# Row tiles 2 and 3 normalised in 64-row halves, tiles 4 and 5 without quarter folding, W1's upper copy loaded once

## The chip, the cores and the metric

The kernel runs on one core of a Trainium2 chip. The time is the device time of one execution in microseconds (us); lower is better. The core has a matrix engine (PE, with its weight loader shown as PEld), a vector engine (DVE), a scalar engine (ACT), GpSimd (POOL) and SyncE (SP), which here only issues transfers. Each engine works through its own queue in order and waits on semaphores for the others. On-chip data lie in SBUF (128 partitions); matmul results land in PSUM, eight banks of 128 x 512 float32 values.

## The reference

The input x has 2048 rows of 448 bf16 values. Two kinds of layer alternate, twice each:

```python
def _A_ref(x, w_r, w_i):                      # spectral layer
    X = rfft2(x)                              # over 2048 rows and 448 columns
    return irfft2(X * (w_r + 1j * w_i))
def _B_ref(x, w1, b1, w2, b2):                # feed-forward layer, 448 -> 1792 -> 448
    h = x @ w1 + b1
    r = where(h > 0, h, 0)
    return (r * r) @ w2 + b2
x = x + _A_ref(_layernorm(x), A_w_r, A_w_i)
x = x + _B_ref(_layernorm(x), B_w1, B_b1, B_w2, B_b2)
x = x + _A_ref(_layernorm(x), A_w_r, A_w_i)
x = x + _B_ref(_layernorm(x), B_w1, B_b1, B_w2, B_b2)
```

The layer normalisation takes the mean and the variance of each row; it has no learned scale.

## The kernel before, in words

The 2048 rows form 16 row tiles of 128 rows (row 16p + t lies in partition p of tile t). Everything stays in SBUF from the first load to the last store. One pass consists of a spectral layer and a feed-forward layer, and the kernel makes two passes.

The spectral layer is a chain of small matmuls against constant matrices. `first_A` (or `second_A` in the second pass) does a part of the transform over rows, `stage_TD` the transform over the 448 columns (called d), `stage_B` the rest of the rows, `stage_W` multiplies by the spectral weights on DVE, and `stage_Bi` begins the inverse. The end of the inverse works tile by tile, two tiles at a time from tile 2 on: `stage_TI` (line 1087) is the inverse transform along d, whose result ACT or DVE copies from PSUM to `TIo`; `stage_AI` (line 1109) is the last step over rows, after which DVE adds the result to x (line 1146). For tiles with `t >= LATE[L]`, here 4, both steps use "quarter folding": `stage_TI` computes only 112 of 224 columns per matmul, four DVE operations of sums and differences (lines 1124 and 1127) make the rest, and `stage_AI` then streams 224 columns per matmul where it otherwise streams 448.

The feed-forward layer begins with `ln_B` (line 1164). It sums the squares of each row (line 1170) and takes a square root on ACT. Then there are two ways. Tiles 0 to 3 are left unnormalised: the standard deviation is written into two spare columns beside x, so that the matmul adds b1 times the deviation, and the layer's result is scaled afterwards with `r2`, the squared reciprocal. Tiles 0 and 1 are transposed on PE (`flip`), tiles 2 and 3 by a transposing transfer on SP's queue. Tiles 4 to 15 go through `ln_rows` (line 1211): reciprocal, one scaling per tile (on ACT or DVE), a copy of the last 64 columns, and the transposing transfer into `yT`. The array has 128 rows, and 448 columns of x make three blocks of 128 and one of 64.

The first matmul of the layer, called h, works on a chunk of four tiles and 14 blocks of W1's columns. For chunk 0 it is `h_part` (line 1266), on two tiles (256 columns) at a time, with four full-height matmuls per block, of which the fourth has data in half of its rows only. For the other chunks it is `h_pairs` (line 1226), on four tiles (512 columns), with seven matmuls of 64 rows per block; the matmuls of two blocks alternate between the lower and the upper half of the array. The upper half needs W1's last 64 rows a second time, in partitions 64 to 127: that copy is `W1u`, which before lies in the memory of `VT` (the inverse's work tensor) and is loaded by two transfers on SP's queue in each pass, after tile 6's transpose. ACT evicts each block with a ReLU (line 1277 or 1254, recorded as line 700), DVE squares it (recorded as line 735), and `o_tile` (line 1280) multiplies each tile by W2 in 14 matmuls and adds x on DVE (line 1292).

The order of each engine's instructions is written out in full. Work is cut into units, each engine's order is a list of unit numbers in `ORDER` (line 115), and `_Sched.schedule` (line 349) follows these lists; the costs and priorities in the code serve only where no list is given. Where its costs leave a long gap on PE, the planner also puts in dummy matmuls on `ones` (line 1415) to keep PE's activity up. Because the numbers are given in the order in which units are created, any change of the code renumbers all later units.

```python
# before, line 1369: chunk 0, two tiles at a time
for t0, t1 in ((0, 2), (2, 4)) if c == 0 else ():
    h_part(c, range(4 if t0 == 0 else 1), t0, t1)
    for fb in range(4 if t0 == 0 else 1, FB):
        h_part(c, (fb,), t0, t1)
```

## Time and profile before

| What | Value |
|---|---|
| time, median of 3 runs | 267.29 us (266.42 to 267.77) |
| the profiled execution's own time | 267.07 us |
| its span, first to last instruction | 265.1 us |
| PE busy | 257.7 us (97%) |
| DVE busy | 204.1 us (77%) |
| ACT busy | 172.8 us (65%) |
| share of PE in the chain that ended last | 80% |
| mean granted PE clock | 1.00 |

How to read the profile. The table of groups gives for each kind of instruction its engine, what it writes and reads, its shape, count, busy time, mean duration, and the idle time of the engine before it with what ended that. The chain that ended last is followed back from the last instruction: at each step to the instruction that released it. The timeline merges neighbouring instructions of one kind: start, time to the end of the last one, count. Nearly all matmuls are recorded under line 681, nearly all DVE operations on two tensors under 735, plain copies by ACT under 706 and by DVE under 707, so groups are told apart by their tensors: `ps<-yT,W_sb` is h, `ps<-yT,VT` is h with W1's upper copy, `ps<-W_sb,arena` is the second matmul, `ps<-TI_sb,VT` is `stage_TI` and `ps<-tmp,FI_sb` is `stage_AI`. In this kernel `arena` holds the squared h, the spectral work tensors and the normalised rows in turn.

### The profile page before, as it was taken

What the parts mean: (1) busy time and instruction counts of PE and PEld (TensorE: products, weight loads), DVE (VectorE), ACT (ScalarE), POOL (GpSimd) and SP (SyncE); (2) the same over time, 40 slices, a digit from 0 to 9 for tenths busy, and PEclk for the clock granted to TensorE, in tenths of its full rate; (3) what the DMA queues carried; (4) which work ended last, traced back from release to release, by engine and by line L of the source; (5) the groups of instructions that cost most, each with busy time, mean ns of one, the idle gap of its engine ahead of it and who ended that gap; (6) DMA issues with size and microseconds to landing.
All of it is one profiled execution on the core that took longest, in us unless ns stands there. A gap on an engine that the chain in (4) does not pass through costs nothing.

```text
span 265.1 us, 5674 instructions
## 1 busy us (share of the span) xinstructions
PE 257.7 (97%) x2127; PEld 163.0 (61%) x2127; DVE 204.1 (77%) x658; ACT 172.8 (65%) x375; POOL 14.3 (5%) x32
## 2 busy tenths in 40 slices
PE   8999989999999999999999999999999999999996
PEld 2686768797544555665558756789654465554454
DVE  3878998999969983489998899899964069921662
ACT  5887897999449447893216889999634886121820
POOL 8840000000000000000000000000000000000000
PEclk9999999999999999999999999999999999999999
DMA  7999700032300224000000000022232000220053
GB/s 226 383 262 350 262 3 2 0 72 41 74 2 1 42 39 80 2 0 2 0 1 2 2 0 2 0 45 41 42 69 45 2 0 2 40 41 2 0 176 104
DMA packets 25531, 16.33 MB, mean 62 GB/s; under 512 B 18174, under 2 KB 24542, under 8 KB 25504
## 3 DMA queue, kind: packets, MB, share of 16 engines
q1 hardware_dynamic: 24768, 14.25, 20.5%
q10 hardware_dynamic: 576, 0.92, 1.0%
q0 software_dynamic: 160, 0.81, 0.8%
q8 instruction: 17, 0.28, 0.5%
q14 instruction: 10, 0.08, 0.1%
HBM read 10.46 MB, written 1.84 MB: 46 GB/s over the span
## 4 chain that ended last, share of the span: by engine, by line
PE 80%; DVE 9%; ACT 6%; DMA 3%; issue 1%; SPq 1%; DVEq 0%
PE ps L681 80%; DVE tmp L735 6%; DMA xin<-in_A_x_dram 3%; DVE arena L735 2%; ACT VT L706 2%; ACT tmp L706 2%; ACT arena L706 2%; SPq L673 1%; DVE st L825 0%; ACT yT L706 0%; ACT mv L700 0%; PE ps L1415 0%; ACT Fs L717 0%; DVE VT L707 0%; DVE x_sb L1292 0%
## 5 line engine op out<-in xcount | busy, mean ns | idle before, releaser
L681 PE MATMUL ps<-yT,W_sb 64*128 64x512 bf16 (+1 forms) x770 | 90.3, 346 | 0.1
L681 PE MATMUL ps<-W_sb,arena 128*128 128x448 bf16 (+3 forms) x476 | 87.0, 342 | 0.0
L681 PEld LDWEIGHTS ps<-yT,W_sb 64*128 64x128 bf16 (+1 forms) x770 | 54.5, 95 | 31.9 <-ACT arena L700 1.3
L700 ACT ACTIVATE arena<-ps,b1col 128x512 bf16<-128x512 f32 x84 | 51.9, 689 | 28.7 <-PE ps L681 28.6
L681 PEld LDWEIGHTS ps<-W_sb,arena 128*128 128x128 bf16 x476 | 45.4, 98 | 38.5 <-DVE arena L735 1.5
L735 DVE TENSOR_TENSOR arena<-arena 128x512 bf16<-128x512 bf16 (+1 forms) x140 | 45.5, 362 | 24.7 <-ACT arena L700 24.5
L706 ACT ACTIVATE arena<-ps 128x448 bf16<-128x448 f32 (+1 forms) x41 | 26.0, 705 | 4.8 <-PE ps L681 4.7
L1170 ACT ACTIVATE VT<-x_sb 128x448 bf16<-128x448 bf16 x28 | 16.1, 579 | 16.6 <-DVE x_sb L1146 16.6
L700 ACT ACTIVATE mv<-mv,epst 128x1 f32<-128x1 f32 (+1 forms) x45 | 12.5, 296 | 17.0 <-DVE mv L826 14.0
L700 ACT ACTIVATE arena<-ps 128x256 bf16<-128x256 f32 x56 | 18.0, 386 | 0.6 <-PE ps L681 0.5
L681 PE MATMUL ps<-arena,G_sb 128*128 128x448 bf16 (+1 forms) x84 | 16.9, 335 | 0.9 <-ACT arena L706 0.9
L1292 DVE SCALAR_TENSOR_TENSOR x_sb<-ps,mv,arena 128x448 bf16<-128x448 f32 (+2 forms) x13 | 8.3, 643 | 12.0 <-PE ps L681 11.9
L706 ACT ACTIVATE XA<-ps 128x512 bf16<-128x512 f32 x26 | 14.2, 591 | 4.7 <-PE ps L681 4.7
L681 PE MATMUL ps<-H_sb,arena 128*128 128x256 bf16 x128 | 15.8, 273 | 1.2 <-DVE arena L735 0.6
L706 ACT ACTIVATE VT<-ps 128x1024 bf16<-128x1024 f32 (+2 forms) x20 | 14.0, 772 | 3.0 <-PE ps L681 3.0
L681 PE MATMUL ps<-yT,VT 64*128 64x512 bf16 x42 | 15.8, 376 | 0.0
L735 DVE TENSOR_TENSOR tmp<-arena,Wt 128x896 bf16<-128x896 bf16 x26 | 15.3, 620 | 0.6 <-ACT arena L706 0.4
L681 PEld LDWEIGHTS ps<-H_sb,arena 128*128 128x128 bf16 x128 | 11.7, 98 | 5.0 <-DVE arena L735 3.4
L681 PE MATMUL ps<-TD_sb,XA 112*128 112x112 bf16 (+3 forms) x232 | 14.4, 230 | 0.3 <-ACT arena L706 0.2
L681 PEld LDWEIGHTS ps<-TD_sb,XA 112*128 112x128 bf16 (+3 forms) x232 | 12.3, 103 | 3.1 <-ACT arena L706 0.8
L706 ACT ACTIVATE tmp<-ps 128x896 bf16<-128x896 f32 (+1 forms) x16 | 12.7, 853 | 1.1 <-PE ps L681 1.0
L681 PEld LDWEIGHTS ps<-arena,G_sb 128*128 128x128 bf16 x84 | 7.7, 98 | 6.5 <-ACT arena L706 1.5
(84 smaller groups left out, 299.0 us busy)
## 6 DMA issues: line engine op xcount, KB each, us to landing
out_dram<-x_sb SPq DMA_DIRECT2D x15, 112.0 KB, 1.8
W_sb<-in_B_w_dram SPq DMA_DIRECT2D x1, 1568.0 KB, 12.9
W_sb<-in_B_w_dram SPq DMA_DIRECT2D x1, 1344.0 KB
xin<-in_A_x_dram ACTq DMA_DIRECT2D x4, 224.0 KB, 5.2
xin<-in_A_x_dram SPq DMA_DIRECT2D x4, 224.0 KB, 7.2
H_sb<-c_H SPq DMA_DIRECT2D x1, 896.0 KB, 8.2
G_sb<-c_G SPq DMA_DIRECT2D x1, 672.0 KB, 9.5
Wt<-in_A_w_i_dram SPq DMA_DIRECT2D x1, 393.8 KB, 5.5
```

What stands on the lines that cost most here:

```text
L673: return e.dma_start(o, i)
L681: return sch.add("pe", lambda e: e.matmul(_res(o), lhsT, rhs, start=start, stop=stop, skip_group_check=skip), [lhsT, rhs], [o], cost=cost, ...
L700: sch.add("act", lambda e: e.activation(o, _res(i), func, **kw), rd, [o], cost=c)
L706: op = sch.add(engs[0], lambda e: e.activation(o, _res(i), ACT.Copy) if h[0].eng == "act" else e.tensor_copy(o, _res(i)), [i], [o], cost=c ...
L735: sch.add(eng, lambda e: e.tensor_tensor(o, _res(a), b, op), [a, b], [o], cost=_free(o) / rate + 69.0)
L1170: op = sch.add("act", lambda e, i=i, o=o, x=x, h=h: e.activation(o, x, ACT.Square, accum_out=sd[:, i, 1:2]) if h[0].eng == "act" else e.sc ...
L1292: small(lambda e: e.scalar_tensor_tensor(out=o, in0=_res(i), scalar=rs[0] if rs else 1.0, in1=xi, op0=ALU.add if t >= 4 and last else ALU. ...
```

## The change

Three things change, and all the order lists with them.

1. A constant `RAW = 2` takes the place of the 4 up to which tiles stay unnormalised. Tiles 2 and 3 now go through `ln_rows`, and their part of h goes through `h_pairs`, which gets the tile range as parameters: 64-row matmuls of 256 columns, evicted with b1 as a bias.
2. `LATE` goes from (4, 4) to (6, 6): tiles 4 and 5 take the way without quarter folding.
3. `W1u` becomes a tensor of its own, holds only the seven blocks that are read (every second one), and is loaded once at the start. The two transfers in each pass go away.

In the new lists the order differs in many places. In the first pass PE now does output tiles 0 and 1 before h of tiles 2 and 3, and h of tiles 4 to 7 directly after that, ahead of output tiles 2 and 3; tile 6's `stage_AI` comes before the first h. In the second pass h of tiles 2 and 3 follows h of tiles 0 and 1, then output tiles 3, 2, 0, 1, then h of tiles 4 to 11. Output tile 11 is the first pass's last, where before it was the second half of tile 15. In SP's list W1's two large parts and `W1u` come before the last part of `H_sb`, then W2, then `TI_sb`.

```diff
+RAW = 2
 ORDER = {
     "pe": """
...
-LATE = (4, 4)
+LATE = (6, 6)
...
-        W1u = VT[:].rearrange("p a b t c j -> p (a b) (t c j)")
+        W1u = sb("W1u", [P, FB // 2, P])
...
-        memset(x_sb[:, 0:4, D:4 * P].bitcast(FP32), 0.0, eng="pool")
+        memset(x_sb[:, 0:RAW, D:4 * P].bitcast(FP32), 0.0, eng="pool")
...
+        dma("sp", W1u[64:128], B_w1[384:448, :].rearrange("r (i k c) -> r i k c", k=2, c=P)[:, :, 1, :])
...
-            if t >= 4:
+            if t >= RAW:
                 ln_rows(t, n, last)
                 return
...
-            if t < 4 and last:
+            if t < RAW and last:
...
-        def h_pairs(c):
+        def h_pairs(c, t0, t1):
-            tk = slice(4 * c, 4 * c + 4)
+            tk, w = slice(4 * c + t0, 4 * c + t1), (t1 - t0) * P
...
-                w = W1u[h, fb // 4, fb % 4 * P:(fb % 4 + 1) * P] if up and j == 3 else W1_sb[h, j, f]
-                op = mm(q[fb][lambda b: ps[:, b, :]], w, yT[h, tk, j, :], start, stop, unit=u)
+                k = W1u[h, fb // 2, :] if up and j == 3 else W1_sb[h, j, f]
+                op = mm(q[fb][lambda b: ps[:, b, 0:w]], k, yT[h, tk, j, :], start, stop, unit=u)
...
-                    hb = hbuf[c % 2][:, fb, :]
-                    act(hb, q[fb][lambda b: ps[:, b, :]], ACT.Relu, bias=b1col[:, fb:fb + 1])
+                    hb = hbuf[c % 2][:, fb, t0 * P:t1 * P]
+                    act(hb, q[fb][lambda b: ps[:, b, 0:w]], ACT.Relu, bias=b1col[:, fb:fb + 1])
...
-            rs = [r2[:, t, 0:1]] if t < 4 else [mv2[:, t, 3:4]] if last else []
+            rs = [r2[:, t, 0:1]] if t < RAW else [mv2[:, t, 3:4]] if last else []
...
-                if t == 6:
-                    for k, w in ((0, 3), (3, 1)):
-                        dma("sp", W1u[64:128, k:k + w, 0:min(4 * P, FF - 4 * P * k)],
-                            B_w1[384:448, 4 * P * k:min(FF, 4 * P * (k + w))].rearrange("r (k c) -> r k c", k=w),
-                            after=[yT[:, 6, 0, :]])
...
-                    h_pairs(c)
-                for t0, t1 in ((0, 2), (2, 4)) if c == 0 else ():
+                    h_pairs(c, 0, 4)
+                for t0, t1 in ((0, RAW), (RAW, 4)) if c == 0 else ():
...
+                    if t0 > 0:
+                        h_pairs(c, t0, t1)
+                        continue
+                    h_part(c, range(4), t0, t1)
+                    for fb in range(4, FB):
```

More of the change, by code (lines that the diff above doesn't have):

```diff
@@ L1290, in o_tile @@
             i = q[lambda b: r(ps[:, b, 0:n])]
-            rs = [r2[:, t, 0:1]] if t < 4 else [mv2[:, t, 3:4]] if last else []
+            rs = [r2[:, t, 0:1]] if t < RAW else [mv2[:, t, 3:4]] if last else []
             small(lambda e: e.scalar_tensor_tensor(out=o, in0=_res(i), scalar=rs[0] if rs else 1.0, in1=xi,
-                                                   op0=ALU.add if t >= 4 and last else ALU.mult, op1=ALU.add),
+                                                   op0=ALU.add if t >= RAW and last else ALU.mult, op1=ALU.add),
                   [i, xi] + rs, [o], n / 0.96 + 128.0)
```

15 lines of the change are left out of this document (6 added, 9 removed), and 89 rows, old and new, of the table ORDER.

## The prediction

> **What bounds the kernel now.** I read the page's engine totals first, then the chain that ended last, then the engines' busy time stage by stage, and the timeline only where a stage showed idle time.
>
> ```profile
> span 265.1 us, 5674 instructions
> PE 257.7 (97%) x2127; PEld 163.0 (61%) x2127; DVE 204.1 (77%) x658; ACT 172.8 (65%) x375; POOL 14.3 (5%) x32
> ...
> 50.26 94.14 PE ps L681 x765
> ...
> 172.48 90.27 PE ps L681 x685
> ```
>
> The matrix engine PE is busy for 97% of the span, and two pieces of the chain, 94.14 and 90.27 us, are unbroken matmul work: there only a change in the number or rate of matmuls moves the end. What is left lies between those pieces. The stage table (columns: stretch and its length, then busy time of PE, weight loader, DVE, ACT, POOL, then clock and DMA) shows it:
>
> ```profile
> 30.00:42.00 12.00, 10.99 (x89) 8.04 (x88) 11.77 (x23) 10.16 (x14) 0.00 (x0) 1.00 0.14 52
> 42.00:50.30 8.30, 7.82 (x94) 6.23 (x93) 7.70 (x25) 7.46 (x15) 0.00 (x0) 1.00 0.01 2
> 50.30:65.00 14.70, 14.70 (x132) 12.61 (x133) 14.21 (x48) 14.11 (x47) 0.00 (x0) 1.00 0.25 51
> ...
> 150.00:162.00 12.00, 11.22 (x114) 7.81 (x112) 12.00 (x25) 10.38 (x15) 0.00 (x0) 1.00 0.00 0
> 162.00:173.00 11.00, 10.32 (x113) 8.07 (x111) 9.96 (x28) 10.01 (x17) 0.00 (x0) 1.00 0.01 1
> ```
>
> From 30 to 42 us and from 150 to 162 us DVE is full (11.77 of 12.00, 12.00 of 12.00): that is the multiplication by the spectral weights, which the diff leaves alone but for order. From 42 to 50.3 and 162 to 173 us (the ramps: inverse transform and normalisation of the first tiles until the feed-forward part starts) PE idles 0.48 and 0.68 us by the table, and waits somewhat longer than that, as its busy time counts the tails of matmuls. From 50.3 to 65 us PE is full, and DVE (14.21 of 14.70) and ACT (14.11) nearly are. So the change can act in three ways: by PE work, by the length of the two ramps, and by what falls late in the stretch after the first ramp. The granted clock is 1.00 in every row.
>
> **The change part by part.** The sum is made against the profiled execution, 267.07 us: span 265.1 and 1.97 around it. It lies 0.22 below the median of the three runs (267.29).
>
> First, the matmuls of tiles 2 and 3 in the first layer of the feed-forward part (14 blocks).
>
> ```profile
> 57.09 6.71 PE L681 MATMUL ps<-yT,W_sb 128*128 128x256 bf16 x60
> ...
> 76.66 1.67 PE L681 MATMUL ps<-yT,W_sb 64*128 64x512 bf16 x13
> 77.96 0.38 PE L681 MATMUL ps<-yT,VT 64*128 64x512 bf16 x1
> 78.17 1.67 PE L681 MATMUL ps<-yT,W_sb 64*128 64x512 bf16 x13
> ...
> 76.45 1.39 PEld L681 LDWEIGHTS ps<-yT,W_sb 64*128 64x128 bf16 x13
> ...
> 46.75 0.49 PEld L681 LDWEIGHTS ps<-TI_sb,VT 112*128 112x128 bf16 x8
> 46.85 0.56 PE L681 MATMUL ps<-TI_sb,VT 112*128 112x112 bf16 x8
> L681 PE MATMUL ps<-yT,W_sb 128*128 128x256 bf16 x224 | 25.9, 273 | 0.1
> ```
>
> Sixty 256-column matmuls take 6.71 us; without the last one's 0.273 that is 109.1 ns each. Today tiles 2 and 3 need 14 x 4 = 56 of them: 6.11 us. After, they need 14 x 7 = 98 matmuls of 64 rows, two at a time. At 512 columns such a pair takes (78.17 - 76.66) / 7 = 216 ns, the time of 512 columns streamed once, so the halves do run side by side. If they do at 256 columns too, 49 pairs at 109.1 ns take 5.35 us: 0.76 us less in each of the two passes. The doubt is the weight loads, two to a pair in half the time. Loads of 128 columns follow each other here every (0.49 - 0.098) / 7 = 56 ns, so even one after the other two take 112 ns: 5.49 us, a gain of 0.62. If pairs didn't overlap at all at this width, 98 x 109.1 = 10.69, a loss of 4.58. I take -0.76, because the rows of pairs are the nearest. The accumulation of a bank changes halves after four pairs of other work (0.44 us at this width); a matmul's 0.273 fits in that.
>
> By the Trainium skill, "TensorE: Matmul & The Clock Gate", section "LDWEIGHTS (loading the stationary operand)", a load takes its columns divided by 1.2 in ns whatever the rows, 107 ns for 128 columns; if the two loads of a pair went in sequence at that price, the pair would take 213 ns and the stage 49 x 213 = 10.5 us, 4.3 us more per pass (an estimate from that page). The trace disagrees on the rate: 56 ns between loads.
>
> Second, tiles 4 and 5 without quarter folding. The first step's eight matmuls get 224 columns in place of 112, the second step's four get 448 in place of 224.
>
> ```profile
> 46.46 0.55 PE L681 MATMUL ps<-tmp,FI_sb 128*128 128x224 bf16 x4
> ...
> 47.95 0.93 PE L681 MATMUL ps<-tmp,FI_sb 128*128 128x448 bf16 x4
> ...
> L681 PE MATMUL ps<-tmp,FI_sb 128*128 128x224 bf16 x64 | 8.6, 260 | 0.0
> L735 DVE TENSOR_TENSOR VT<-tmp 128x448 bf16<-128x448 bf16 x24 | 8.9, 382 | 0.1
> L735 DVE TENSOR_TENSOR tmp<-VT 128x448 bf16<-128x448 bf16 x24 | 8.6, 383 | 0.1
> L718 DVE TENSOR_SCALAR arena<-x_sb,rstd 128x448 bf16<-128x448 bf16 x15 | 4.7, 328 | 2.7 <-DMA yT<-arena 2.7
> L739 DVE COPY arena<-arena 128x128 bf16<-128x128 bf16 x12 | 2.3, 191 | 1.0 <-ACT arena L717 0.7
> ```
>
> The second step costs 0.93 - 0.55 = +0.38 us. A 224-column matmul takes (0.55 - 0.260) / 3 = 97 ns, a 112-column one (0.56 - 0.213) / 7 = 50 ns, so the first step costs 8 x 47 = +0.38. Together +0.76 per pass: what the halves give on PE, this takes back, and PE's own work stays as it is to within 0.1 us. On DVE four operations of 0.382 go, -1.53 us per pass; normalising tiles 2 and 3 adds two scalings (0.328), a copy (0.191) and a reciprocal (about 0.16) and drops four operations of about that length (two for the bias rows, two for the scale of the output), so DVE has about 1.2 us less per pass, in the stretch where it is nearly full.
>
> Third, W1's upper copy. It moves from two transfers in each pass to one transfer at the start (64 rows of 7 x 128 columns, 112 KB), queued on SP ahead of the last spectral constants.
>
> ```profile
> 70.10 1.31 SPq L673 DMA_DIRECT2D VT<-in_B_w_dram  x2
> ...
> VT<-in_B_w_dram SPq DMA_DIRECT2D x2, 192.0 KB, 3.3
> 42.74 1.75 PE L681 MATMUL ps<-TI_sb,VT 112*128 112x224 bf16 x22 [0.20 <-DVE VT L707]
> ```
>
> The 192 KB transfer landed in 3.3 us; I charge the new one at most that, in a start whose transfers are idle in the 30 to 42 us row but for a share of 0.14. The constant put last in SP's queue is the inverse matrix, first used at 42.74. Cost 0. The removed transfers held SP for 1.31 us in a pass, ahead of transposes for tiles that PE needs much later, so 0 there too; if the cover at the start went, it would cost up to 3.3.
>
> Fourth, ACT. The half-height path adds b1 as a bias on the eviction.
>
> ```profile
> L700 ACT ACTIVATE arena<-ps,b1col 128x512 bf16<-128x512 f32 x84 | 51.9, 689 | 28.7 <-PE ps L681 28.6
> L700 ACT ACTIVATE arena<-ps 128x256 bf16<-128x256 f32 x56 | 18.0, 386 | 0.6 <-PE ps L681 0.5
> L706 ACT ACTIVATE XA<-ps 128x512 bf16<-128x512 f32 x26 | 14.2, 591 | 4.7 <-PE ps L681 4.7
> ```
>
> With a bias 689 ns, without one 591 at the same size: 98 ns more, 14 times, 1.4 us of ACT per pass (0 at the lower end). Evictions overlap: 18.0 / 56 = 321 ns each, so about 419 with bias, against 5.35 / 14 = 382 that PE needs per block. ACT falls behind by 14 x 37 ns = 0.5 us, which the eight PSUM banks hold. Cost 0, up to 0.7 per pass if no bank is free.
>
> Fifth, the new order, which is where an unshown cost can be. In the first ramp the order puts tile 6's second step (0.38) and the longer tiles 4 and 5 (0.76) ahead of the first h matmul, and on ACT one more 896-wide eviction between the square roots and the transposed tiles' evictions.
>
> ```profile
> 43.74 4.96 ACT L706 ACTIVATE tmp<-ps 128x896 bf16<-128x896 f32 x6 [0.51 <-PE ps L681]
> 48.55 0.52 ACT L700 ACTIVATE mv<-mv,epst 128x1 f32<-128x1 f32 x2
> 48.92 1.58 ACT L706 ACTIVATE yT<-ps 128x384 bf16<-128x384 f32 x4
> ```
>
> Six such evictions take 4.96 us, 0.83 each. ACT would then reach the transposed tiles at about 48.55 + 0.52 + 0.83 = 49.9 and finish their two large pieces (0.45 each) at 50.8: h starts near 50.9 instead of 50.26, 0.64 later with 1.14 us more of PE work behind it. Gain 0.5; I take -0.4, as the small pieces come after a square on ACT. Bounds: -1.0 (all waiting in the ramp gone), +1.0 (nothing absorbed). In the second ramp by the same steps PE has 1.5 us more work ahead of h (0.76, and 0.76 of tiles 4, 14 pulled forward) and h starts about 1.65 later: +0.15, between -0.7 and +1.0. The stage with 64-row matmuls is entered once more in the second pass; around such a switch the loader idled 0.37 us, 0.19 of it under the last matmul:
>
> ```profile
> 74.92 0.54 PEld L681 LDWEIGHTS ps<-yT,W_sb 64*128 64x128 bf16 x7 [0.37 <-issue]
> 144.34 0.61 PE L1415 MATMUL ps<-ones 128*128 128x512 bf16 x2
> ```
>
> So about 0.1 a switch, +0.2 for two (0 to 0.4). The Trainium skill, "TensorEngine Tiling (Array Packing)", section "Key Properties", says that changing the tiling mode drains the engine; by that the switch has a price too, and the row agrees. Tiles 2 and 3 reach their transpose later, behind a reciprocal, two scalings and a copy:
>
> ```profile
> 53.44 1.34 SPq L668 DMA_TRANSPOSE yT<-x_sb  x1
> ...
> 176.03 1.23 SPq L668 DMA_TRANSPOSE yT<-x_sb  x1
> ...
> 172.95 0.27 PE L681 MATMUL ps<-yT,W_sb 128*128 128x256 bf16 x1
> ```
>
> In the first pass two output tiles (14 matmuls each) now stand between the h blocks of tiles 0, 1 and 2, 3, which leaves over 4 us. In the second nothing does: with the ramp's 1.65 and about 0.7 for the added steps the issue moves from 176.03 to about 178.4, the landing (3 us) to 181.4, and PE, which starts h at 172.95 + 1.65 = 174.6, gets there at 174.6 + 6.11 + 0.76 = 181.5. So it just fits: 0, up to +1.0.
>
> Between the passes the order ends the first on a whole tile (11) rather than on half of tile 15; PE fills there with dummy matmuls already (144.34), so the longer last chain shows: +0.1, between 0 and 0.6. The spectral stages keep their DVE work: 0, within 0.3.
>
> Sum: -1.52 + 1.52 - 0.4 + 0.15 + 0.2 + 0.1 = +0.05, so 267.1 us. Its own range is 265.8 to 268.4, this kernel's 0.5% (1.34 us), which is also about what a measurement can tell from no change.
>
> **The rivals.** Faster, because DVE binds the ramps. For it: DVE is at 7.70 of 8.30 and 9.96 of 11.00 there and loses 1.2 us in each pass. Against it: what it loses stood mostly after the critical squares, and ACT is just as full. If both ramps lost their waits, -1.0 and -0.7 in place of -0.4 and +0.15, and the 42 to 65 us stretch gave a further half us through earlier tiles, the time would be 265.1 to 265.6; I write 265.3.
>
> Slower, because tiles 4 to 7 come late. The order starts their h block straight after tiles 2 and 3, ahead of output tiles 2 and 3, and so about 6 us earlier than today (74.92), near 68.4. Their transposes are issued today at 60.64 and about 67:
>
> ```profile
> 60.64 7.64 SPq L668 DMA_TRANSPOSE yT<-arena  x2
> yT<-arena SPq DMA_TRANSPOSE x12, 3.0
> ```
>
> They land 3.0 us after issue. The second must be issued by 65.4; a count of DVE's operations ahead of it gives about 65.2. From there each us of DVE delay is one of PE: +1.5 us for a transpose issued at 67 as today gives 268.7. For it: DVE and ACT at 96% there. Against it: DVE's 1.2 us less.
>
> Slower, because ACT's bias paces the block in both passes: 2 x 0.7, 268.5. Slower by far, because pairs do not overlap at this width: 2 x (4.58 + 0.76) = +10.7, 277.8; the 512-column rows speak against it. The page's load rule would do the same at 2 x (4.3 + 0.76), 277.
>
> **How the numbers follow.** The forecast 0.47, DVE-bound ramps 0.28, late tiles 0.16, ACT's bias 0.06, no overlap 0.03. So faster by over 0.5% 0.28, within 0.5% 0.47, slower 0.25. The range 265.0 to 269.0 takes in the first two rivals' bounds and leaves out no overlap and the far ends.
>
> **What would show it.** Right: the 64-row matmuls of 256 columns at some 110 ns a pair; PE's busy time within 1 us of 257.7; h starting near 50.9 and 1.65 us later in the second pass. Wrong: PE waiting on a transpose or on ACT's evictions near 64 to 70 us; pairs over 115 ns; ramps shorter than today; or PE gaps before 42 us from late constants.

## The result and the profile after

Medians of twenty runs each on the same chips: 267.56 us after (267.29 to 268.60), 266.44 us before (266.20 to 267.77). The ratio is 1.0031, with a 95% interval from 1.0021 to 1.0041: the change costs 0.8 us by that ratio, 1.1 us between the two medians. The forecast was a difference of +0.05 us, and the interval leaves that out. That the absolute number, 267.1, came nearer than the difference is luck: its base lay high, as the profiled execution of before, 267.07 us, is 0.6 us above what that kernel takes in the median of twenty.

The page of the changed kernel, totals:

```profile
span 265.6 us, 5871 instructions
...
PE 256.6 (97%) x2212; PEld 160.0 (60%) x2212; DVE 202.1 (76%) x649; ACT 174.3 (66%) x375; POOL 14.1 (5%) x32
```

PE is busy 1.1 us less than before, DVE 2.0 us less, and the kernel is longer all the same. The chain that ended last (start, length, what) says where to look:

```profile
50.38 19.72 PE ps L680 x197
70.10 1.26 ACT arena L699 x2
71.41 69.91 PE ps L680 x525
141.34 1.57 ACT XA L705 x3
...
143.09 0.77 ACT XA L705 x2
143.91 0.90 PE ps L680 x20
...
167.12 95.89 PE ps L680 x794
```

Before, one piece of 94.14 us of matmuls reached from the first h to the end of the first pass. Now it is broken twice: at 70.10 by two of ACT's evictions, and at 141.34 by the chain at the end of the pass. The second pass is one piece of 95.89 us, longer than the 90.27 of before, as it now begins already in the ramp. The stage table (stretch, length, busy time of PE, weight loader, DVE, ACT, POOL, clock, DMA):

```profile
42.00:50.30 8.30, 7.94 (x92) 6.56 (x92) 7.88 (x24) 7.38 (x16) 0.00 (x0) 1.00 0.01 2
50.30:65.00 14.70, 14.63 (x130) 10.84 (x131) 14.24 (x51) 10.14 (x34) 0.00 (x0) 1.00 0.20 39
150.00:162.00 12.00, 11.78 (x124) 8.68 (x122) 12.00 (x25) 10.97 (x16) 0.00 (x0) 1.00 0.00 1
162.00:173.00 11.00, 10.16 (x104) 7.86 (x103) 10.51 (x27) 8.79 (x14) 0.00 (x0) 1.00 0.01 1
```

In the first of these stretches PE is busier than before (7.94 of 8.30, it was 7.82); ACT is relieved from 50 to 65 us (10.14, it was 14.11); the spectral stage is full on DVE as it was.

The two profiled executions can't be laid side by side by their clocks, because PE's first matmuls of the transform along d start at different times. The rows of that start and of the last matmuls, before:

```profile
17.52 1.76 PE L681 MATMUL ps<-TD_sb,XA 128*64 128x224 bf16 x32
...
257.81 4.93 PE L681 MATMUL ps<-W_sb,arena 128*128 128x448 bf16 x39
```

and after:

```profile
16.89 1.76 PE L680 MATMUL ps<-TD_sb,XA 128*64 128x224 bf16 x32
...
257.69 5.31 PE L680 MATMUL ps<-W_sb,arena 128*128 128x448 bf16 x41
```

From the start of the transform to the last matmul's end it is 257.81 + 4.93 - 17.52 = 245.22 us before and 257.69 + 5.31 - 16.89 = 246.11 after: +0.89. The start itself lies between 16.7 and 17.6 us in the kernels below, without any order among them, while three kernels whose PE work is the same (after, and the second and third experiment, e2_nobias and e4_squares) agree to 0.03 us in this length. So it is used from here on as the length of PE's work, cut into six stages by the start times of the matmuls named here (in us): transform up to the first matmul of `stage_TI`; first ramp up to the first h; h 1 up to the last first-step matmul of the next pass's spectral layer; spectral stage of the second pass; second ramp; second h to the end.

| Kernel | transform | ramp 1 | h 1 | spectral 2 | ramp 2 | h 2 | sum |
|---|---|---|---|---|---|---|---|
| before | 25.22 | 7.53 | 93.95 | 22.65 | 6.08 | 89.78 | 245.21 |
| after | 25.11 | 8.38 | 93.70 | 23.05 | 7.43 | 88.43 | 246.10 |
| e13_no_mix_only | 25.11 | 8.38 | 93.31 | 23.05 | 7.43 | 88.43 | 245.71 |
| e7_no_mix | 25.10 | 8.37 | 93.24 | 23.03 | 7.43 | 88.44 | 245.61 |
| e6_halves_last | 25.10 | 8.37 | 93.97 | 22.81 | 7.43 | 88.44 | 246.12 |
| e9_offload | 25.09 | 8.37 | 93.33 | 22.86 | 7.43 | 88.44 | 245.52 |
| e11_evac | 25.10 | 8.37 | 93.33 | 22.73 | 7.43 | 88.43 | 245.39 |
| p2_unfolded | 25.22 | 7.92 | 93.95 | 22.66 | 6.46 | 90.18 | 246.39 |
| p1_w1u_once | 25.22 | 7.52 | 93.95 | 22.66 | 6.08 | 90.48 | 245.91 |
| e12_folded | 25.10 | 8.13 | 95.47 | 22.72 | 7.33 | 89.88 | 248.63 |
| e3_order | 25.22 | 7.92 | 95.84 | 22.65 | 6.46 | 91.03 | 249.12 |

From the second ramp on the change gains nothing and loses nothing (ramp 2 and h 2 together 95.86 in both). The loss is made before: ramp 1 and h 1 together are 102.08 us after and 101.48 before, and spectral 2, which begins with what the end of the pass has left over, is 0.40 longer.

### The profile page after: what moved, and what is told of

The parts are those of the page before. It is cut to its first block, busy times and chain, and to the rows that moved or that the text cites. A ratio compares the mean times of both kernels' runs of the same rounds, so it can differ in the third digit from the quotient of the medians.

```text
span 265.6 us, 5871 instructions
## 1 busy us (share of the span) xinstructions
PE 256.6 (97%) x2212; PEld 160.0 (60%) x2212; DVE 202.1 (76%) x649; ACT 174.3 (66%) x375; POOL 14.1 (5%) x32
## 4 chain that ended last, share of the span: by engine, by line
PE 78%; DVE 15%; ACT 2%; issue 2%; DMA 1%; DVEq 0%
PE ps L680 77%; DVE tmp L734 9%; DVE arena L734 3%; DMA xin<-in_A_x_dram 1%; ACT arena L705 1%; ACT XA L705 1%; PE ps L1413 1%; DVE st L825 1%; DVE x_sb L1146 1%; DVE VT L706 1%; ACT arena L699 0%; DVE VT L1171 0%; DVE tmp L706 0%; DVE VT L734 0%; DVE arena L706 0%
## 5 line engine op out<-in xcount | busy, mean ns | idle before, releaser
L699 ACT ACTIVATE arena<-ps,b1col 128x512 bf16<-128x512 f32 (+1 forms) x112 | 63.7, 634 | 39.0 <-PE ps L680 38.8
L680 PE MATMUL ps<-yT,W_sb 64*128 64x512 bf16 (+2 forms) x840 | 88.7, 339 | 0.1
L680 PEld LDWEIGHTS ps<-yT,W_sb 64*128 64x128 bf16 (+1 forms) x840 | 51.2, 94 | 34.5 <-issue 1.9
L1292 DVE SCALAR_TENSOR_TENSOR x_sb<-ps,mv,arena 128x448 bf16<-128x448 f32 (+2 forms) x15 | 9.5, 649 | 14.0 <-PE ps L680 13.8
L705 ACT ACTIVATE XA<-ps 128x512 bf16<-128x512 f32 (+1 forms) x27 | 14.6, 585 | 7.7 <-PE ps L680 7.5
L680 PE MATMUL ps<-yT,W1u 64*128 64x512 bf16 (+1 forms) x56 | 19.6, 349 | 0.0
L699 ACT ACTIVATE mv<-mv,epst 128x1 f32<-128x1 f32 (+1 forms) x45 | 12.7, 299 | 9.6 <-DVE mv L826 9.3
L1170 ACT ACTIVATE VT<-x_sb 128x448 bf16<-128x448 bf16 x28 | 16.2, 581 | 2.1 <-DVE x_sb L1146 2.1
L705 ACT ACTIVATE VT<-ps 128x1024 bf16<-128x1024 f32 (+2 forms) x19 | 13.3, 801 | 1.9 <-PE ps L680 1.9
L680 PE MATMUL ps<-tmp,FI_sb 128*128 128x224 bf16 (+1 forms) x72 | 10.7, 280 | 0.3 <-DVE x_sb L738 0.3
L1146 DVE SCALAR_TENSOR_TENSOR x_sb<-ps,mv,x_sb 128x448 bf16<-128x448 f32 x16 | 10.5, 678 | 0.3 <-PE ps L680 0.3
```

The source lines that it names most:

```text
L680: return sch.add("pe", lambda e: e.matmul(_res(o), lhsT, rhs, start=start, stop=stop, skip_group_check=skip), [lhsT, rhs], [o], cost=cost, ...
L699: sch.add("act", lambda e: e.activation(o, _res(i), func, **kw), rd, [o], cost=c)
L705: op = sch.add(engs[0], lambda e: e.activation(o, _res(i), ACT.Copy) if h[0].eng == "act" else e.tensor_copy(o, _res(i)), [i], [o], cost=c ...
L1146: small(lambda e, xx=xx, xi=xi, r=r, m=m: e.scalar_tensor_tensor(out=xx, in0=_res(r), scalar=m, in1=xi, op0=ALU.subtract, op1=ALU.add), [r ...
L1170: op = sch.add("act", lambda e, i=i, o=o, x=x, h=h: e.activation(o, x, ACT.Square, accum_out=sd[:, i, 1:2]) if h[0].eng == "act" else e.sc ...
L1292: small(lambda e: e.scalar_tensor_tensor(out=o, in0=_res(i), scalar=rs[0] if rs else 1.0, in1=xi, op0=ALU.add if t >= RAW and last else AL ...
```

## The experiments

In the order lists below, o11 is output tile 11 (14 matmuls), o15' and o15'' are the halves of tile 15, F9 the first-step matmuls of tile 9 for the next spectral layer, T0 to T3 the first four groups of `stage_TD`, h23 and h47 the h matmuls of tiles 2, 3 and 4 to 7, numbered by unit (two blocks each).

**Three edits that follow the chain's rows.** The chain names two places, so each was mended first as it reads. At the end of the pass, with the order of the kernel before:

```diff
 PE, end of the first pass (DVE and ACT alike)
-o10 F8 o15' o15'' o11 F13 F9 F14 T0 F10 F12 F15 F11 T2 T1 T3
+o10 o11 F8 o15' F9 o15'' F10 F14 F12 T0 F13 T2 F11 F15 T3 T1
```

> The changed kernel with one thing undone: from output tile 10 of the first pass to the first matmuls of the second spectral layer, PE, DVE and ACT take the order of the kernel before (whole tile 11 ahead of the halves of tile 15). The changed kernel stands 1.1 us above the kernel before (267.56 against 266.44). Theory order-tail: the 0.8 us that PE waits at 142.7 us for tile 11's chain go, so it comes out 0.6 to 0.8 us under the changed kernel, +0.3 to +0.5 against the kernel before. Rival absorbed: the stage after it is full on DVE, so an earlier PE gains nothing there; then it stays within 0.2 us of the changed kernel, +0.9 to +1.3 against the kernel before, and the idle time turns up after 145 us.

Measured: 269.90 us against 266.54, ratio 1.0128 (1.0107 to 1.0150). Neither theory: 2.3 us worse than the changed kernel. DVE's timeline shows why (the bracket holds the idle time before the operation and what ended it):

```profile
138.57 0.26 DVE L717 TENSOR_SCALAR Fs<-FA_sb,rstd 128x128 bf16<-128x128 bf16 x1 [2.39 <-PE ps L680]
```

DVE stood idle for 2.39 us, waiting for PE ahead of an operation placed for another neighbourhood, and the kernel came out 2.3 us longer. An order list is good only together with what surrounds it; and in this run DVE's idle time went into the length of the kernel almost whole.

At 70 us, without the bias on the evictions of tiles 2 and 3 (b1 is left out for these two tiles; the evictions of h47 keep theirs):

```diff
-act(hb, q[fb][lambda b: ps[:, b, 0:w]], ACT.Relu, bias=b1col[:, fb:fb + 1])
+act(hb, q[fb][lambda b: ps[:, b, 0:w]], ACT.Relu, **({} if c == 0 else {"bias": b1col[:, fb:fb + 1]}))
```

> The changed kernel without the bias on ACT's evictions of h of tiles 2 and 3, in both passes (b1 is left out for these two tiles). Theory bias: with it an eviction takes 395 ns against 382 that PE needs for a block, without it about 320, so ACT keeps up, the waits of 1.1 us and less of PE at 70 to 71.4 us go, and the time falls by 0.4 to 0.5 us, +0.6 to +0.7 against the kernel before. Theory squares: the two squares of ACT that stand between these evictions make the lag; then the 14 x 75 ns saved leave some of the wait and the time falls by 0.1 to 0.3 us. If neither paces PE, the time stays within 0.1 us.

and with two squares moved ahead of them:

```diff
 ACT, first pass
-... scale(t6), evict h23 0 3 2 5 1 7 6 9, square(t9), 4 8, square(t11), ..., square(t10), ...
+... scale(t6), square(t9), square(t10), evict h23 0 3 2 5 1 7 6 9 4 8, ..., square(t11), ...
```

> The changed kernel with ACT's order changed in one place of the first pass: the squares of tiles 9 and 10 (0.65 us each) go ahead of the first eviction of h of tiles 2 and 3, where ACT idles 1.85 us, and the square of tile 11 takes the later place of that of tile 10. So two squares less stand between the evictions from 65.4 to 71.4 us. Theory squares: PE's waits for ACT at 70 to 71.4 us go, the time falls by 0.4 us, to +0.7 against the kernel before. Theory bias: the evictions alone are too slow at 395 ns, some of the wait stays, the time falls by at most 0.2 us.

Measured: 267.57 us without the bias (ratio to before 1.0033, 1.0021 to 1.0045) and 267.65 with the squares moved (1.0038, 1.0024 to 1.0053): nothing gained by either. Without the bias the chain doesn't even name ACT any more:

```profile
51.03 90.94 PE ps L680 x742
```

and yet PE loses the same time: in all three kernels it resumes 54.5 us after the start of the transform. Neither the bias on these evictions nor the two squares are the cause. Both order edits together:

```diff
 the two order edits above together
```

> Both changes of order together (end of the first pass as in the kernel before, squares of tiles 9 and 10 ahead of the evictions). If order alone makes the loss and the two add, 1.1 to 1.2 us under the changed kernel, that is 0 to -0.1 us against the kernel before. If one of them is absorbed, only the other one's gain is left: +0.4 to +0.7. If the code of the change itself costs, it stays 0.5 us or more above the kernel before whatever the order.

Measured: 270.08 us against 266.54, ratio 1.0128 (1.0109 to 1.0148): the loss of the first edit, and nothing from the second.

**The banks.** What the three have in common is what PE and ACT do at that place. In the changed kernel:

```profile
64.89 0.92 PE L680 MATMUL ps<-yT,W_sb 64*128 64x256 bf16 x13
65.66 0.92 PE L680 MATMUL ps<-yT,W_sb 64*128 64x256 bf16 x13
...
65.42 2.77 ACT L699 ACTIVATE arena<-ps,b1col 128x256 bf16<-128x256 f32 x7 [0.26 <-PE ps L680]
...
71.38 0.42 DVE L734 TENSOR_TENSOR arena<-arena 128x512 bf16<-128x512 bf16 x1 [4.80 <-ACT arena L699]
```

The order begins h47 (unit 0, four blocks of 512 columns) between units 4 and 5 of h23. With these four and the last four blocks of h23 all eight banks are taken, and by the bank numbers that the order assigns, unit 1 of h47 gets the banks of h47's first two blocks: it must wait until ACT has evicted both, 0.69 us for one of them, and ACT can't start on them before PE has finished them. How fast ACT was with the blocks ahead of these two is of no matter, and the run without the bias shows it: there ACT is early and stands idle for PE before it can evict the two.

```profile
70.74 1.26 ACT L699 ACTIVATE arena<-ps,b1col 128x512 bf16<-128x512 f32 x2 [0.33 <-PE ps L680]
```

In both kernels these two evictions begin 53.2 us after the start of the transform and take 1.26 us. (In the changed kernel DVE waits at the same place for 4.80 us, because its list too has a square of h47 ahead of those of h23.) The test is to undo the mixing alone:

```diff
 PE, first pass (ACT and DVE alike)
-h23.0 h23.1 h23.2 h23.3 h23.4 h47.0 h23.5 h23.6 h47.1 ...
+h23.0 h23.1 h23.2 h23.3 h23.4 h23.5 h23.6 h47.0 h47.1 ...
```

> The changed kernel with one change of order only: h of tiles 4 to 7 starts after the last pair of h of tiles 2 and 3, on PE, ACT and DVE; the squares of ACT stay between the evictions. With the squares moved as well it gained 0.5 us. Theory banks: the mixing alone was the loss, -0.4 to -0.5 us against the changed kernel, +0.5 against the kernel before. Theory ACT: without the mixing ACT's two squares (1.3 us) and the evictions at 372 ns a block let PE run out of banks a little later instead, and there is no gain, or a wait of up to 0.6 us at the second pair of tiles 4 to 7: +0.9 to +1.2.

and with the squares moved too:

```diff
 the edit above, and the squares of tiles 9 and 10 ahead of the evictions
```

> The changed kernel with h of tiles 4 to 7 starting only after the last pair of h of tiles 2 and 3 (PE, ACT and DVE), and the squares of tiles 9 and 10 ahead of the evictions. Taking away the bias or two squares had moved nothing: PE resumed at the same time after the start of its work (54.51 us) in all three, when the first 512-column block of tiles 4 to 7 had been evicted. Theory banks: all eight banks are taken because that chunk is begun between pairs 5 and 6 of the other; without the mixing the 0.3 us of waiting at 71 us go, and the time falls by 0.2 to 0.3 us, to +0.8 against the kernel before. Rival: ACT is behind anyway at 372 ns a block and PE waits as long a little later; no change. Rival DVE-full: DVE sets the end of the pass; no change although the wait at 71 us goes.

Measured: 267.22 against 266.61 for the first (ratio 1.0021, 1.0010 to 1.0032), 267.00 against 266.60 for the second (1.0019, 1.0010 to 1.0028). In the length of PE's work that is -0.39 and -0.49 us to the changed kernel, nearly all of it in the column h 1. The chain of the first is whole again at that place:

```profile
50.39 90.55 PE ps L680 x743
```

The theory of the banks holds: the mixing alone cost 0.39 us. The squares add 0.1 us, once PE no longer waits for something else. Whether faster evictions of h47's own blocks would have shortened the wait was not tried.

**The end of the pass.** Here the changed kernel has its whole tile 11 last, and PE waits for that tile's statistics and normalisation. PE's and DVE's rows in its timeline:

```profile
140.92 0.83 PE L680 MATMUL ps<-Fs,tmp 128*128 128x128 bf16 x12
...
142.89 0.38 PE L1413 MATMUL ps<-ones 128*128 128x512 bf16 x1
143.91 0.38 PE L680 MATMUL ps<-Fs,tmp 128*128 128x128 bf16 x4 [0.64 <-ACT XA L705]
...
144.74 0.50 PE L1413 MATMUL ps<-ones 128*128 128x512 bf16 x2
145.17 1.87 PE L680 MATMUL ps<-TD_sb,XA 112*64 112x112 bf16 x48
...
141.12 0.62 DVE L1292 SCALAR_TENSOR_TENSOR x_sb<-ps,arena 128x448 bf16<-128x448 f32 x1
...
143.56 0.25 DVE L717 TENSOR_SCALAR Fs<-FA_sb,rstd 128x128 bf16<-128x128 bf16 x1
```

Tile 11's chain on DVE runs from 141.12 to 143.81, 2.7 us, and PE has work for 2.0 us from 140.92 on, and then a dummy matmul. The wait is put down to ACT, whose evictions end at 143.86 by the chain's row; DVE's last scaling ends 0.05 us before that, so the row doesn't decide between the two. Dummies counted as idle time, PE has none of the program's work from 142.89 to 143.91 and from 144.74 to 145.17, 1.45 us. Before, PE ran on to the end and was without work only from 144.34 to 145.01, 0.67 us:

```profile
139.97 4.43 PE ps L681 x80
...
144.34 0.61 PE L1415 MATMUL ps<-ones 128*128 128x512 bf16 x2
145.01 1.87 PE L681 MATMUL ps<-TD_sb,XA 112*64 112x112 bf16 x48
```

This time DVE's list was arranged for the new order:

```diff
 PE (DVE: operations of tiles 11 and 15 interleaved to match; ACT alike)
-o10 F8 o15' o15'' o11 F13 F9 F14 T0 F10 F12 F15 F11 T2 T1 T3
+o10 F8 o11 o15' o15'' F13 F9 F14 T0 F10 F12 T2 F11 F15 T1 T3
```

> The changed kernel (1.1 us above the kernel before) with the end of its first pass ordered anew on PE, DVE and ACT: output tile 11 straight after tile 10, then the two halves of tile 15, so that the last chain through statistics and normalisation is that of a half tile; PE gets the first-step matmuls of tiles 13, 9, 14, 10, 12 and two of the four first groups of the next stage as cover. DVE's list is arranged so that it doesn't idle (in the run where the order of the kernel before was put in, DVE idled 2.39 us at 136.1 us and the end came 2.3 us later). Theory chain: the 0.8 us in which PE waits at 142.7 us for tile 11's chain are the loss; they go, and with two groups of the next stage done earlier the time falls by 0.6 to 0.9 us, to +0.2 to +0.5 against the kernel before. Theory DVE-full: DVE is busy 25.80 of 26 us from 118 to 144 us and has the same work in any order; the end moves by less than 0.2 us, +0.9 to +1.2.

Measured: 267.59 against 266.60 (1.0041, 1.0028 to 1.0055), no gain. The rows before the last matmuls now read:

```profile
135.97 7.44 PE ps L680 x94
143.41 0.15 DVE rstd L856
143.58 0.27 DVE Fs L717
```

The half tile's chain is shorter, and the wait for it falls to 0.64 us; but PE then runs dummies for longer before the next stage's matmuls, and its time without work is 1.50 us in all, as in the changed kernel. My reading is that DVE gets to the last tiles no earlier, as it does the same work in either order. Both edits together:

```diff
 e7_no_mix and e6_halves_last together
```

> Both together. If the chain at the end of the pass and the bank wait at 71 us are separate losses of PE, 0.8 to 1.2 us under the changed kernel: -0.1 to +0.3 against the kernel before. If DVE's load from 118 us on sets the end of the pass, no more than 0.2 us: +0.9.

Measured: 267.18 against 266.60 (1.0025, 1.0011 to 1.0039): what the banks give, and no more. So is it DVE's load? Nine scalings go to ACT:

```diff
-EV = {..., 'FS2': ['dve'], ...}
+EV = {..., 'FS2': ['act', 'dve'], ...}
 order lists: scalings of the first-step matrix for tiles 3, 4, 7, 8, 9, 10, 12, 13, 14 from DVE's to ACT's
```

> The run with both changes of order (no mixing of the two h blocks, squares early, tile 11 ahead of the halves of tile 15; +0.6 us against the kernel before), and in addition nine of the scalings of the first-step matrix by a tile's reciprocal deviation (128x128, about 0.16 us of DVE's pace each) move from DVE to ACT, which is busy 11.07 of 26 us from 118 to 144 us. The arithmetic stays. Theory DVE-full: that stretch ends when DVE's work is done; 9 x 0.16 = 1.4 us less on DVE end it earlier until PE is the limit again, and the time falls by 0.4 to 0.9 us, to +0.2 to -0.3 against the kernel before. Theory chain: the end hangs on the latency of the last tile's chain alone, and the time stays within 0.15 us of the run without the move.

> The same nine scalings on ACT, but with the end of the first pass in the changed kernel's order (halves of tile 15 first, whole tile 11 last; without the move +0.4 us against the kernel before). There DVE waits about 0.1 us for tile 11's matmuls before the last chain, so PE as well as DVE sets its start. Theory DVE-full alone: as good as the other order, -0.4 us or more. Theory balance: DVE gets done with the rest earlier but the last chain can't start before PE ends tile 11; 0 to -0.2 us, +0.2 to +0.4 against the kernel before.

The first run makes this move in e8_both (halves last), the second in e7_no_mix (whole tile last). Measured: 267.06 against 266.50 with the halves last (1.0019, 1.0009 to 1.0030), 267.08 with the whole tile last (1.0016, 1.0005 to 1.0026). In PE's length that is -0.16 and +0.01 us to the same orders without the move (245.68 and 245.61). The stretch from 118 to 140 us in e8_both, and then with the move:

```profile
118.00:140.00 22.00, 22.00 (x145) 12.58 (x141) 21.80 (x103) 8.37 (x21) 0.00 (x0) 1.00 0.00 1
```

```profile
118.00:140.00 22.00, 22.00 (x146) 13.12 (x145) 20.78 (x94) 10.80 (x29) 0.00 (x0) 1.00 0.01 1
```

DVE is relieved by 1.0 us (21.80 to 20.78), and PE stays full. That DVE's load over the whole stretch sets the end, which would have brought 0.4 us or more, is not borne out. But DVE isn't cleared either: with the halves last the chain runs on DVE from a reciprocal at 135.99 to the last scaling, with nothing but DVE's rows between. If that chain is the whole story, what is left hangs on DVE's work on the last tiles; no run shortened that work.

```profile
135.99 0.16 DVE rstd L855
...
143.07 0.27 DVE Fs L716
143.43 0.39 PE ps L679 x8
```

ACT was the third candidate, with four evictions in a row at the end; this edit stands on e9_offload:

```diff
 order lists: first half of tile 15's first-step eviction from ACT's to DVE's
```

> The run with both changes of order and nine scalings on ACT (+0.5 us against the kernel before), and one eviction more moved: the first half of tile 15's first-step result goes from ACT, where it stands behind four evictions of 0.48 us in a row at the end of the pass, to DVE, as in the kernel before. Theory ACT's queue: after tile 15's last matmul ACT is still 0.4 us behind, which holds up the last two groups of the next stage; moved, the time falls by 0.2 to 0.4 us, to +0.1 to +0.3 against the kernel before. If the last chain on DVE alone sets the end, it stays within 0.1 us or loses the 0.3 us of the eviction.

Measured: 266.77 against 266.39 (1.0015, 1.0006 to 1.0024); in PE's length -0.13 us. And more work for PE behind the last output tile, on top of that:

```diff
 PE (ACT alike)
-o14 F4 F3 o9 o10 F8 o11 o15' o15'' F13 ...
+o14 F3 o9 o10 o11 o15' F8 o15'' F4 F13 ...
```

> The best order so far (no mixing, squares early, tile 11 ahead of the halves of tile 15, nine scalings on ACT, one eviction back on DVE; +0.2 us in length of the PE work, +0.4 us measured against the kernel before) with the first-step matmuls of tiles 8 and 4 (0.26 us each) moved from ahead of output tile 11 to behind the first and the second half of tile 15. The chain of the last two tiles then starts 0.5 us earlier on DVE, and PE has 0.5 us more to do while it runs; in the run without it PE waits 0.45 us for the last scaling. Theory cover: PE's cover behind the last output tile is what is short; 0.3 to 0.45 us less, level with the kernel before to within 0.2 us. Theory DVE: DVE has no idle time left ahead of the chain and can't start it earlier; no gain.

Measured: 277.36 against 266.61 (1.0396, 1.0376 to 1.0415). The edit makes a wait of its own:

```profile
140.48 0.65 DVE L733 TENSOR_TENSOR tmp<-xin 128x224 bf16<-128x224 bf16 x3 [11.43 <-PE ps L679]
```

DVE writes tile 12's sums where tile 4's stand, and F4 now reads those 11 us later. So the cover that was wanted can't be had by delaying F4; the question whether cover is what is short was not answered by this run.

**The parts.** W1's upper copy alone, in the kernel before:

```diff
-W1u = VT[:].rearrange("p a b t c j -> p (a b) (t c j)")
+W1u = sb("W1u", [P, FB // 2, P])
+dma("sp", W1u[64:128], B_w1[384:448, :].rearrange("r (i k c) -> r i k c", k=2, c=P)[:, :, 1, :])
-                if t == 6:
-                    for k, w in ((0, 3), (3, 1)):
...
```

> The kernel before with one part of the change alone: W1's upper copy in memory of its own, loaded once at the start after the last spectral constant; the two transfers in each pass go. The prediction priced it at 0: within 0.2 us of the kernel before. If the start is delayed by the added transfer, up to +3.3; if SP's 1.3 us per pass held up transposes, a gain of 0.3 or more.

Measured: 267.28 against 266.50 (1.0021, 1.0006 to 1.0036): a loss, in the column h 2 alone (+0.70). The chain of that run:

```profile
175.37 4.91 DMA yT<-x_sb
```

The transposing transfer of tiles 2 and 3 in the second pass lands 4.9 us after its issue, where the kernel before, and the changed kernel, need 3.1 for these tiles. What the traces show of the reason stands in the last section; the changed kernel doesn't pay this loss.

Tiles 4 and 5 unfolded alone, in the kernel before:

```diff
-LATE = (4, 4)
+LATE = (6, 6)
 order lists: without the four DVE operations of tiles 4, 5 in each pass
```

> The kernel before with another part alone: tiles 4 and 5 without quarter folding, their four DVE operations per pass left out of the order, all else as it was. The prediction priced it at +0.76 us of PE per pass: +1.5 us if PE sets the pace in both passes. Rival: the four operations (0.38 us each) go from a DVE that is full in the ramps, so the ramp waits shrink by as much: +0.4 to +0.8. If DVE alone bounds the ramps, a gain.

Measured: 267.87 against 266.50 (1.0047, 1.0031 to 1.0062); in PE's length +1.17 us: 0.39 in the first pass, 0.78 in the second, so between the two first theories. The second ramp, before and then with the part, shows the full price and no more waiting than before:

```profile
172.48 0.57 PE L681 MATMUL ps<-TI_sb,VT 112*128 112x112 bf16 x8
172.89 0.22 PE L681 MATMUL ps<-J_sb,x_sb 128*128 128x128 bf16 x1
```

```profile
172.44 0.94 PE L681 MATMUL ps<-TI_sb,VT 112*128 112x224 bf16 x8
173.22 0.22 PE L681 MATMUL ps<-J_sb,x_sb 128*128 128x128 bf16 x1
```

The eight matmuls take 0.94 in place of 0.57 us. In the first ramp PE's own work grows by 0.75 us, and the ramp by 0.39: there the waits become shorter by the difference, as the rival said.

The whole code in the order of the kernel before:

```diff
 after.py with the order lists of before.py: units that are gone left out; the reciprocal, the two
 scalings and the copy of tiles 2, 3 in place of the copy of the deviation; b1's columns ahead of h23
```

> The whole code of the change (64-row halves for tiles 2 and 3, tiles 4 and 5 unfolded, W1's upper copy once) with the order lists of the kernel before carried over: what the code no longer has is left out, the reciprocal, the two scalings and the copy of tiles 2 and 3 stand where the copy of the deviation stood, and b1's columns are made before the first eviction that needs them. Theory order: the code is neutral within its price terms (-0.76 and +0.76 per pass) and only the written order lost; then 0 to +0.7 against the kernel before, with waits for the transposes of tiles 2 and 3, which that order places early. Theory code: the code itself costs, +1 us or more.

Measured: 270.70 against 266.60 (1.0156, 1.0142 to 1.0169), far from the theory of order, and by its number on the side of the theory of code. The loss is in h 1 (+1.9) and h 2 (+1.25), and the waits of the first pass aren't for transposes, as I had expected, but for ACT:

```profile
54.48 0.94 ACT arena L699 x3
55.42 0.55 ACT VT L1170 x2
...
61.00 1.22 ACT arena L716 x2
```

The evictions (L699) that PE waits for stand behind squares (L1170) and the scalings of tiles 4 and 5 (L716) on ACT, which that order put there for a kernel whose h23 took PE longer. So code and order can't be priced apart: the code needs lists of its own, and those of the change lose 3 us less than the old ones.

The folding put back into the best of the mended kernels:

```diff
-LATE = (6, 6)
+LATE = (4, 4)
 on e11_evac; the four DVE operations behind those that lead to the first h, the second step behind h's first unit
```

> The same as the run before it, with one part of the change undone: tiles 4 and 5 take quarter folding again in both passes, their four DVE operations standing behind the operations that lead to the first h matmul, and their second step behind the first unit of h. Unfolding put alone into the kernel before came 1.17 us later from the start of the transform to the end. Theory price: what is left of the loss is the price of unfolding in the two ramps, 0.4 us in the first pass and 0.8 in the second; then 0.8 to 1.2 us less than the run before it, -0.5 to -0.9 against the kernel before, faster than both kernels. Rival DVE: the 1.5 us per pass of DVE come back in the stretch behind the ramps where it is nearly full, and make the transposed tiles late; no gain or a loss.

Measured: 269.99 against 266.39 (1.0138, 1.0122 to 1.0153), 3.2 us longer in PE's work. The rival is right: DVE's operations come back where the normalisation of tiles 2 and 3 now needs DVE too. PE idles for DVE behind the ramp, and does 13.65 us of work in a stretch that it filled with 14.63:

```profile
50.30:65.00 14.70, 13.65 (x103) 9.38 (x100) 13.67 (x49) 9.82 (x33) 0.00 (x0) 1.00 0.23 37
...
54.29 1.91 PE L680 MATMUL ps<-yT,W_sb 128*128 128x256 bf16 x16 [0.59 <-DVE rstd L1215]
```

So the first two parts of the change hang together, at least in the one order tried: the halves' normalisation costs DVE part of what the unfolding spares it. No version tried was faster than the kernel before; the best, e11_evac, lies 0.15% above it.

## Why the prediction was wrong

**The halves.** Right. A pair of 64-row matmuls of 256 columns takes (65.66 - 64.89) / 7 = 0.110 us, as forecast (109.1 ns). The Trainium skill's rule in "TensorE: Matmul & The Clock Gate", section "LDWEIGHTS (loading the stationary operand)", by which the two loads of a pair, one after the other, would need 213 ns, isn't borne out here either.

**The unfolded tiles.** Right in kind. Priced at +0.76 per pass, measured alone +0.39 and +0.78; together with the halves PE's matmul work comes out even to within 0.1 us, as forecast. The unfolding alone cost less than its price in the first ramp, where shorter waits made up for 0.36 us of it.

**The ramps.** In the first pass h starts 0.74 us later, counted from the start of the transform; 0.64 was forecast. The ramp itself is 0.85 us longer with 1.14 us more work in it, so its waits fell by 0.3 where 0.4 was forecast. The second ramp is 1.35 us longer with 1.52 us more work, where 1.65 was forecast: 0.2 gained, and not 0.15 lost.

**The switch.** Forecast +0.2 for two. In the second pass PE loses 0.19 us more than before at the two ends of the added stretch of 64-row matmuls.

**W1's upper copy.** Forecast 0; in the changed kernel nothing of it is seen. Alone it cost 0.70 us, by a slow landing that had no place in the sum.

**ACT, the fourth step: the first that failed.** It read "ACT falls behind by 14 x 37 ns = 0.5 us, which the eight PSUM banks hold. Cost 0, up to 0.7 per pass if no bank is free." The cost was 0.39 us in the first pass, 0.49 with the squares that then count, and the bound takes it in; the mechanism was another. ACT didn't fall behind: with the bias seven evictions took 2.77 us, about 0.38 each as later ones overlap, which is what PE needs for a block, and without it nothing was gained. The prediction had named PE waiting for ACT's evictions near 70 us as a sign of being wrong, and the chain shows that wait, at 70.10. The banks didn't hold because the new order takes them for the next chunk while the old one is still open. I had read from the diff that h47 begins close to h23 and checked only whether its transposed tiles are there; I had not counted how many banks are open at the point where the two meet.

**The end of the first pass, in the fifth step: the second that failed.** It read "the longer last chain shows: +0.1, between 0 and 0.6". PE's time without work there grew by 0.78 us, from 0.67 to 1.45. The step was mis-sized: a whole tile's statistics and normalisation take DVE 2.7 us, and PE had 2.0 us of work to cover them. What sets this end isn't shown. Order alone gives nothing, nine scalings off DVE 0.16 us at most, one eviction off ACT 0.13. Of the 0.89 us of PE's length, 0.49 goes with the banks (and the squares behind them) and 0.22 with these edits of the end; 0.18 stays, and whether PE's cover or DVE's chain holds it is open. With these two terms at 0.49 and 0.78, the switch at 0.19, and 0.1 us gained in the transform, 0.3 in the first ramp and 0.2 in the second, the sum gives 0.9, which is the loss that was measured.

**The first view.** Both failures go against a sentence in the first part of the prediction: that in the unbroken pieces of the chain "only a change in the number or rate of matmuls moves the end". A piece is unbroken as long as the engines behind PE keep up and a bank is free, and from 118 us on DVE had 0.3 us to spare in 22 even before:

```profile
118.00:140.00 22.00, 22.00 (x140) 12.38 (x136) 21.71 (x104) 7.48 (x18) 0.00 (x0) 1.00 0.00 1
```

The piece of 94.14 us broke where the order became tighter. The rival about late tiles had its eye on that region, but on the wrong resource: nothing waited for the transposes.

**The forecast's own range** (265.8 to 268.4) holds 267.56, and so does the whole one. But what it said was no change, and the kernel is slower by an interval that leaves no change out. From the base of 266.44 its own range would have been 265.2 to 267.8, which still holds the result.

## What to carry to other kernels

Where an order begins a second producer of PSUM blocks before the first is drained, count the open banks at that point: speeding up the evictions ahead of it doesn't help when the next matmul's bank belongs to a block that has only just been finished. A chain that shows PE unbroken for 90 us doesn't say that PE alone sets the time; look how much the engine behind it has to spare in the same stretch before you price a shift of work at its PE time. And when two profiled executions are compared, take lengths from a common point of the work, not clock times: here the start alone moves by as much as the effect.

## What the hardware showed that I had not expected

One transposing transfer of the same size took 4.9 us to land in p1_w1u_once, in the profile of the second pass:

```profile
yT<-x_sb SPq DMA_TRANSPOSE x1, 4.9
```

against this in the kernel before:

```profile
yT<-x_sb SPq DMA_TRANSPOSE x1, 3.1
```

In the records of the transfer queues its 1056 packets take 2.6 us in place of 1.5, the longest 305 ns in place of 91, and a 16 KB fetch of instructions (0.88 us) runs from 178.22 us within that time; in the kernel before the fetch begins only at 178.52, 0.15 us ahead of the packets' end.

The other traces bear the link out. The eighteen profiles hold 224 transposing transfers of this size whose landing can be told. The 169 that had no fetch of instructions in the time of their packets all landed within 3.3 us; of the 55 that had one, 29 took 3.6 us or more, up to 4.9. The changed kernel has a slow one too (4.1 us, issued at 102.26 us in the first pass), but nothing waits for it. No run moved a fetch and kept all else, so that the fetch is the cause remains an inference. The loss of this part alone stood in the median of twelve runs; that it comes from where the fetch falls is argued, not shown.
